# Copying and splitting a pair's first keys before, not after, the turning of its centroid products

## The chip, the cores and the metric

One NeuronCore of one Trainium2 chip runs the whole program. The metric is the device time of one execution in microseconds; the time of the kernel before is the median of three runs.

## The reference

A clustered attention, two batches of eight heads, 768 tokens and 64 features a head, is followed by two feed-forward networks. A query sees only the keys that fall to the same of 16 centroids.

```python
q_assign = argmax((q / |q|) @ (c / |c|).T)          # c: 16 centroids of the head
k_assign = argmax((k / |k|) @ (c / |c|).T)
mask = q_assign[:, :, :, None] == k_assign[:, :, None, :]
scores = where(mask, q @ k.T / sqrt(64), -1e9)
attn = softmax(scores) @ v
x = attn with the heads side by side                # 1536 x 512
h = relu(x @ w_in) ** 2 @ w_out                     # 512 -> 2048 -> 512
h = gelu_like(h @ w2_in) @ w2_out                   # 512 -> 2048 -> 512
```

All is float32. The kernel keeps that accuracy by splitting a factor into a high half in the fast format fp32r and a low half, the remainder.

## The kernel before

The heads are worked in eight pairs (pair 0 to pair 7), each pair two heads of the same batch. A pair has 12 steps of 128 query rows, six for each head, and the two heads alternate. One step multiplies a query tile with all 768 keys (`scores`, lines 620 and 623: the high halves against each other first, then the low halves together with 16 mask rows), takes the negative of the row maximum on VectorE (`peak`, line 629), the exponentials on ScalarE (`exponents`, line 637), turns them on TensorE (`turn`, line 645), copies them out of PSUM (`keep`, line 653, on ScalarE or VectorE) and multiplies them with the values (`values`, line 663). The scores have two PSUM buffers: a score needs the exponentials of the score two before it to be done. Most other products share a ring of four PSUM buffers.

While the steps of one pair run, the next pair is prepared (`prep`, from line 439). Its raw keys and queries come by DMA. Then:

- `square` (line 474, GpSimd) squares them, `aff` (lines 481 and 484, TensorE) multiplies with the centroids and sums the squares, `aff_out` (line 490, ScalarE) copies that out of PSUM.
- `back` (line 498, TensorE) transposes these centroid products, `back_out` (line 508, ScalarE) copies the transposes out.
- `root` (line 512, GpSimd) takes the square root of the norms, `inv_norm` (lines 518 and 519, VectorE) adds 1e-6 and inverts, `scale` (line 531, GpSimd) applies it, `most` (line 539, VectorE) takes the maximum over the centroids; `less`, `first`, `least`, `one_hot` (lines 542 to 557) make the assignment, `mask` (line 564) turns it, and DMAs lay it under the queries and keys.
- `k_high(j)` for head j of the pair (line 448, ScalarE) copies the keys into the high half and sends a copy of that by DMA to the other 64 partitions (line 449, SyncE's queue). `k_low(j)` (line 453, GpSimd) subtracts it from the raw keys. `q_high` (lines 458 and 459) and `q_low` (line 463) do the same for the queries. The buffers hold four heads, so the even head of pair p writes where the even head of pair p - 2 was read, by `scores`, to the end of that pair.

Beside this, the attention's results leave: `inverse`, `turn_sums` (lines 673 to 677, VectorE) and `send` (line 682, GpSimd, four small copies) bring the inverse row sums into a row, DMAs of lines 683 and 689 spread them, `whole` (line 722) applies them, `whole_high` and `whole_low` (lines 730 and 734) split the result, and `t_sum_first` (line 741, mostly GpSimd) adds results for the first network. From step 70 on, the networks' weights are decoded too (from line 266). Behind the attention the networks run on TensorE (lines 835, 912, 921 and 1024).

No scheduler decides the order. Each piece of work is put into a list with a number, its moment, by `at`, and the list is sorted; every engine then works its own share of it in that order, and waits where an operand isn't there yet:

```python
start = NQ * p                      # NQ = 12, one unit is one score
at(start + key, f, x)               # key from PAIR, for pairs 3 to 7
begin = ORIGIN + 2 * k              # scores 2k and 2k + 1; ORIGIN = -1.0
GROUP = dict(scores=(0.0, 0.3), peak=(0.5, 0.7), exp=(0.85, 1.5), turn=(2.64, 2.85, 3.06), ...)
for _, _, f in sorted(events, key=lambda e: e[:2]):
```

So the numbers of `PAIR` are moments of a pair's preparation, counted from the start of its own scores. Pair 2 takes `PAIR` too, with some moments of its own (`THIRD`: its `back` is at -15.1 and its `back_out` at -14.75 and -14.7). Pairs 0 and 1 have tables of their own.

Of the kernel before, what the change touches and what calls it, by code (L numbers as in the profile page):

```python
# [32 lines left out]
PAIR = dict(  # L33
    load_q=-20.601, load_k=-20.501, load_v=-5.2, square=(-16.9, -16.5),
    aff=(-15.15, -15.1), aff_out=(-14.95, -14.8), back=(-13.15, -13.1), back_out=(-12.95, -12.8),
    k_high=(-13.4, -6.9), k_low=(-12.95, -6.3), q_high=(-12.6, -10.7), q_low=(-12.2, -8.9),
    root=-12.7, inv_norm=-9.95, scale=-9.9, most=-8.98, less=-8.95, first=-6.98,
    least=-6.95, one_hot=-6.0, mask=(-5.15, -5.1), mask_out=(-4.95, -4.8),
)
# [8 lines left out]
    q_low=(-49.9, -49.8), k_low=(-47.95, -49.7),  # L48
# [8 lines left out]
    q_high=(-11.3, -6.18), q_low=(-10.1, -6.1), k_high=(-5.45, -4.75), k_low=(-5.4, -4.7),  # L57
# [1159 lines left out]
```

## Time and profile before

| | |
|---|---|
| median of three runs | 757.31 us (757.30 to 757.36) |
| the profiled execution | 757.72 us |
| its span, first to last instruction | 755.9 us |
| TensorE busy | 741.3 us, 98% of the span |
| VectorE busy | 530.5 us, 70% |
| ScalarE busy | 454.8 us, 60% |
| GpSimd busy | 173.0 us, 23% |
| granted TensorE clock | 1.00 |

Pair 2 is prepared from about 35 to 58 us of the span, pair 5 from about 124 to 147, pair 7 from about 183 to 210; the attention's steps end near 247 us. In the rows below PE is TensorE, PEld its weight load, DVE VectorE, ACT ScalarE and POOL GpSimd; "arena" is the SBUF area that holds nearly all tiles, and L518 is line 518. The spans of POOL are rough; starts are firmer than ends.

### The profile page before, as it was taken

To read this page: it belongs to the slowest core of one execution; us is meant where nothing else is said; L and a number is where in the kernel's file an instruction comes from. 1 tells how busy PE (TensorE), PEld (TensorE's weight loads), DVE (VectorE), ACT (ScalarE), POOL (GpSimd) and SP (SyncE) were. 2 spreads that over 40 slices of the span, in tenths; PEclk is the share of its full clock that TensorE was granted. 3 is DMA by queue.
4 is the path that set the end of the run, shared out by engine and by line. 5 is a ranking of instruction groups with operands and counts; after the bars stand their busy time and mean duration, and the time that the engine had idled before them with its cause. 6 is when DMAs were issued, how large, how long until landed. Compare 5 with 4: busy or idle time off the path is not lost.

```text
span 755.9 us, 10860 instructions
## 1 busy us (share of the span) xinstructions
PE 741.3 (98%) x3965; PEld 603.5 (80%) x3965; DVE 530.5 (70%) x954; ACT 454.8 (60%) x784; POOL 173.0 (23%) x186
## 2 busy tenths in 40 slices
PE   9899999999999999999999999999999999999998
PEld 6676676676666799999988888888888888888886
DVE  6877877977897667775787769754777677776321
ACT  7877768776777478776844435554656564443321
POOL 4765766785749130000000000000000000000000
PEclk9999999999999999999999999999999999999999
DMA  6143332333321121200232320100212212230301
GB/s 190 47 122 75 97 103 61 87 87 94 108 54 61 69 105 62 108 26 31 83 111 86 109 85 21 36 29 28 84 57 83 84 56 95 101 112 28 112 1 56
DMA packets 19481, 57.53 MB, mean 76 GB/s; under 512 B 3146, under 2 KB 5156, under 8 KB 18404
## 3 DMA queue, kind: packets, MB, share of 16 engines
q1 hardware_dynamic: 19140, 56.19, 23.5%
q8 instruction: 31, 0.51, 0.3%
q10 hardware_dynamic: 288, 0.66, 0.2%
q14 instruction: 22, 0.18, 0.1%
HBM read 45.97 MB, written 3.19 MB: 65 GB/s over the span
## 4 chain that ended last, share of the span: by engine, by line
PE 83%; DVE 7%; ACT 4%; POOL 3%; issue 1%; DVEq 0%; POOLq 0%; ACTq 0%
PE bank L1024 35%; PE row L835 13%; PE bank L912 10%; PE bank L921 6%; PE ps_v L663 5%; PE ps_p L645 5%; DVE arena L629 3%; PE ps_s L620 3%; ACT arena L637 3%; PE ps_s L623 2%; PE ps_aff L481 1%; DVE arena L518 1%; PE ps_h L835 1%; PE warm L397 1%; POOL arena L296 1%
## 5 line engine op out<-in xcount | busy, mean ns | idle before, releaser
L1024 PE MATMUL bank<-arena 128*128 128x512 f32 x1152 | 261.5, 389 | 0.0
L1024 PEld LDWEIGHTS bank<-arena 128*128 128x128 f32 x1152 | 216.1, 188 | 45.0 <-DVE arena L1011 0.2
L637 ACT ACTIVATE arena<-ps_s,arena 128x768 f32<-128x768 f32 x96 | 87.1, 907 | 46.0 <-DVE arena L629 45.9
L629 DVE TENSOR_SCALAR_CACHE_REDUCE arena<-ps_s 128x768 bf16<-128x768 f32 x96 | 91.7, 955 | 32.5 <-ACT arena L490 13.1
L1007 ACT CAST arena<-arena 128x512 fp32r<-128x512 f32 x96 | 59.5, 620 | 85.6 <-PE bank L1024 85.2
L835 PE MATMUL row<-arena 128*128 128x384 f32 x630 | 109.7, 334 | 0.4 <-ACT arena L853 0.4
L835 PEld LDWEIGHTS row<-arena 128*128 128x128 f32 x630 | 109.2, 188 | 0.7 <-ACT arena L853 0.7
L1011 DVE TENSOR_TENSOR arena<-arena,arena 128x512 fp32r<-128x512 f32 x96 | 66.1, 689 | 60.1 <-ACT arena L1007 59.9
L912 PE MATMUL bank<-arena 128*128 128x512 f32 x336 | 80.9, 389 | 0.0
L912 PEld LDWEIGHTS bank<-arena 128*128 128x128 f32 x336 | 63.1, 188 | 13.1
L663 PE MATMUL ps_v<-arena 128*64 128x384 f32 x384 | 72.3, 498 | 0.0
L645 PE MATMUL ps_p<-arena 128*128 128x128 f32 x576 | 70.8, 272 | 0.0
L244 ACT CAST arena<-arena 128x512 fp32r<-128x512 f32 x48 | 29.8, 620 | 64.6 <-DVE arena L240 64.5
L645 PEld LDWEIGHTS ps_p<-arena 128*128 128x128 f32 x576 | 65.8, 141 | 2.2 <-issue 0.6
L620 PE MATMUL ps_s<-arena 128*128 128x384 f32 x192 | 55.1, 368 | 7.0 <-ACT arena L637 6.6
L620 PEld LDWEIGHTS ps_s<-arena 128*128 128x128 f32 x192 | 30.9, 188 | 31.2 <-ACT arena L637 17.3
L247 DVE TENSOR_TENSOR arena<-arena,arena 128x512 fp32r<-128x512 f32 x48 | 33.2, 692 | 24.1 <-ACT arena L244 23.3
L623 PE MATMUL ps_s<-arena 80*128 80x384 f32 x192 | 49.8, 340 | 0.1
L921 PE MATMUL bank<-arena 128*128 128x512 f32 x192 | 48.1, 389 | 0.0
L653 DVE COPY arena<-ps_p 128x512 f32<-128x512 f32 x72 | 47.0, 678 | 0.3 <-PE ps_p L645 0.2
L663 PEld LDWEIGHTS ps_v<-arena 128*64 128x64 f32 x384 | 23.4, 136 | 25.5 <-issue 25.4
L653 ACT COPY arena<-ps_p 128x512 f32<-128x512 f32 x72 | 41.9, 582 | 0.5 <-PE ps_p L645 0.5
(140 smaller groups left out, 939.4 us busy)
## 6 DMA issues: line engine op xcount, KB each, us to landing
arena<-in_w_dram SPq DMA_DIRECT2D x48, 512.0 KB, 3.3
arena<-in_w_dram SPq DMA_DIRECT2D x8, 1024.0 KB, 4.8
arena<-arena SPq DMA_DIRECT2D x32, 192.0 KB, 2.6
arena<-in_k_t_dram SPq DMA_DIRECT2D x8, 384.0 KB, 4.9
arena<-in_v_dram SPq DMA_DIRECT2D x8, 384.0 KB
arena<-sums_d SPq DMA_DIRECT2D x30, 96.0 KB, 2.8
out_dram<-arena SPq DMA_DIRECT2D x11, 256.0 KB, 2.1
arena<-in_q_t_dram SPq DMA_DIRECT2D x7, 384.0 KB, 3.5
```

Of the source, the lines that this page charges most:

```text
L620: nc.tensor.matmul(ps[:, n, :HALF], lhsT=x_s[i][:, t * P:(t + 1) * P], rhs=k1_s[i][:, n * HALF:(n + 1) * HALF], start=True, stop=False)
L623: nc.tensor.matmul(ps[:, n, :HALF], lhsT=q2_s[i][:, t * P:(t + 1) * P], rhs=k2_s[i][:, n * HALF:(n + 1) * HALF], start=False, stop=True)
L629: nc.vector.tensor_scalar(out=unused, in0=s_t[g][:, :, :HALF], scalar1=-scale, scalar2=None, op0=ALU.mult, op1=ALU.min, accum_out=m_t[g])
L637: nc.scalar.activation(out=p_t[g].rearrange("p (n f) -> p n f", n=2), in_=s_t.pop(g)[:, :, :HALF], func=AF.Exp, bias=m_t.pop(g), scale=sca ...
L645: nc.tensor.transpose(ps[:, x * P:(x + 1) * P], p_t[2 * k + j][:, t * P:(t + 1) * P], ident)
L653: (nc.scalar.copy if on_act else nc.vector.tensor_copy)(out=pt_t[n][:, 4 * b:4 * b + 4, i * P:(i + 1) * P], in_=tp_t.pop((k, b)).rearrange ...
L663: nc.tensor.matmul(pv_t[n][j * D:(j + 1) * D, :HALF], lhsT=raw[n // 2, "v"][:, j, t, :], rhs=pt_t[n, j][:, t, :], start=(t == 0), stop=(t ...
L835: nc.tensor.matmul(ps, lhsT=w[:, a, (off + x) * P:(off + x + 1) * P], rhs=FIRST_MOVING[moving, b][x][:, e, :], start=(n == 0 and name in ( ...
L912: nc.tensor.matmul(ps, lhsT=w[:, a, off + x * P:off + (x + 1) * P], rhs=MOVING[moving][x][:, b, :], start=(n == 0 and name in ("P1", "P2", ...
L921: nc.tensor.matmul(ps, lhsT=w[:, a, kk * P:(kk + 1) * P], rhs=THIRD_CHUNK[kk][:, b, :], start=(n == 0), stop=(n == 11), skip_group_check=True)
L1011: nc.vector.tensor_tensor(out=t[:, 1, :], in0=g_t[m][:, c, :], in1=t[:, 0, :].bitcast(F32), op=ALU.subtract)
L1024: nc.tensor.matmul(ps, lhsT=lhsT, rhs=rhs, start=(m == 0 and e == 0), stop=(m == MF - 1 and e == 2))
```

## The change

Two numbers of `PAIR` change, each the moment of the pair's first head (j = 0):

```diff
 PAIR = dict(
-    k_high=(-13.4, -6.9), k_low=(-12.95, -6.3), q_high=(-12.6, -10.7), q_low=(-12.2, -8.9),
+    k_high=(-14.7, -6.9), k_low=(-14.6, -6.3), q_high=(-12.6, -10.7), q_low=(-12.2, -8.9),
```

`back` stands at -13.15 and -13.1, `back_out` at -12.95 and -12.8, `root` at -12.7. The queues of TensorE, VectorE and SyncE stay as they were. On ScalarE and GpSimd the rows of lines 448 and 453 move in pairs 2 to 7.

ScalarE, a preparation as in pairs 3 to 7, before (L490 `aff_out`, L637 exponentials, L653 `keep`, L448 `k_high`, L508 `back_out`, L458 `q_high`):

```order
L490 COPY arena_59<-ps_aff 128x384 x2
L637 ACTIVATE arena_59<-ps_s,arena_59 128x768
L653 COPY arena_59<-ps_p 128x4x128
L637 ACTIVATE arena_59<-ps_s,arena_59 128x768
L448 CAST arena_58<-arena_59 64x768
L653 COPY arena_59<-ps_p 128x4x128
L508 COPY arena_59<-ps_back 128x3x98 x2
L458 CAST arena_58<-arena_59 64x768
```

and now:

```order
L490 COPY arena_59<-ps_aff 128x384 x2
L448 CAST arena_58<-arena_59 64x768
L637 ACTIVATE arena_59<-ps_s,arena_59 128x768
L653 COPY arena_59<-ps_p 128x4x128
L637 ACTIVATE arena_59<-ps_s,arena_59 128x768
L653 COPY arena_59<-ps_p 128x4x128
L508 COPY arena_59<-ps_back 128x3x98 x2
L458 CAST arena_58<-arena_59 64x768
```

The cast of the keys now stands ahead of two exponentials and a copy that it stood behind. In pair 2 it stands between the two copies of line 508.

GpSimd at the same place of pair 5, before (L474 `square`, L734 `whole_low`, L741 `t_sum_first`, L682 `send`, L453 `k_low`, L512 `root`, L463 `q_low`, L531 `scale`):

```order
L474 TENSOR_TENSOR arena_59<-arena_59 128x768 x2
L734 TENSOR_TENSOR arena_58<-arena_59,arena_58 128x384
L741 TENSOR_TENSOR arena_59<-arena_59 128x384 x3
L682 COPY arena_59<-arena_59 6x32 x4
L453 TENSOR_TENSOR arena_58<-arena_59,arena_58 64x768
L512 TENSOR_TENSOR arena_59<-arena_59 128x24
L463 TENSOR_TENSOR arena_58<-arena_59,arena_58 64x768
L531 TENSOR_TENSOR arena_59<-arena_59 128x384
```

and now:

```order
L474 TENSOR_TENSOR arena_59<-arena_59 128x768 x2
L734 TENSOR_TENSOR arena_58<-arena_59,arena_58 128x384
L741 TENSOR_TENSOR arena_59<-arena_59 128x384 x3
L453 TENSOR_TENSOR arena_58<-arena_59,arena_58 64x768
L682 COPY arena_59<-arena_59 6x32 x4
L512 TENSOR_TENSOR arena_59<-arena_59 128x24
L463 TENSOR_TENSOR arena_58<-arena_59,arena_58 64x768
L531 TENSOR_TENSOR arena_59<-arena_59 128x384
```

The subtraction of line 453 went ahead of the four small copies of line 682, and the root follows these directly.

## Rows read from the trace of the kernel before

**Rows 1.** The page, part 1: busy us, share of the span, instructions of TensorE.

```profile
PE 741.3 (98%) x3965; PEld 603.5 (80%) x3965; DVE 530.5 (70%) x954; ACT 454.8 (60%) x784; POOL 173.0 (23%) x186
```

**Rows 2.** Waits of TensorE: waiter, releaser, us in total, times, longest.

```profile
PE ps_s L620 <- ACT arena L637: 6.6, 16, 0.9
```

**Rows 3.** Timeline of TensorE, pair 5: start, length, instruction, [idle before, releaser].

```profile
137.43 1.51 PE L663 MATMUL ps_v<-arena 128*64 128x384 f32 x8
138.87 0.61 PE L620 MATMUL ps_s<-arena 128*128 128x384 f32 x2
...
139.67 0.52 PE L620 MATMUL ps_s<-arena 128*128 128x384 f32 x2
...
141.78 1.51 PE L663 MATMUL ps_v<-arena 128*64 128x384 f32 x8
143.69 0.62 PE L620 MATMUL ps_s<-arena 128*128 128x384 f32 x2 [0.40 <-ACT arena L637]
...
145.06 0.62 PE L620 MATMUL ps_s<-arena 128*128 128x384 f32 x2 [0.41 <-ACT arena L637]
```

**Rows 4.** Chain of waits that ended last, same step: start, us, what.

```profile
138.05 1.73 DVE arena L518
...
142.65 0.99 ACT arena L637 x2
```

**Rows 5.** Timeline of GpSimd and VectorE, pair 5, ahead of that step.

```profile
130.56 0.96 POOL L682 COPY arena<-arena 6x32 f32<-6x32 f32 x4 [2.85 <-ACT arena L448]
131.61 1.82 POOL L453 TENSOR_TENSOR arena<-arena,arena 64x768 fp32r<-64x768 f32 x1
133.39 4.16 POOL L512 TENSOR_TENSOR arena<-arena 128x24 f32<-128x24 f32 x1
137.49 0.55 DVE L734 TENSOR_TENSOR arena<-arena,arena 128x384 fp32r<-128x384 f32 x1
137.63 2.10 POOL L463 TENSOR_TENSOR arena<-arena,arena 64x768 fp32r<-64x768 f32 x1
137.96 1.81 DVE L518 TENSOR_SCALAR arena<-arena 128x24 f32<-128x24 f32 x1
```

**Rows 6.** Timeline of ScalarE and TensorE, pair 5, around the cast's two places.

```profile
124.89 1.05 ACT L490 COPY arena<-ps_aff 128x384 f32<-128x384 f32 x2 [0.65 <-PE ps_aff L484]
125.32 0.62 PE L620 MATMUL ps_s<-arena 128*128 128x384 f32 x2
...
127.46 0.90 ACT L637 ACTIVATE arena<-ps_s,arena 128x768 f32<-128x768 f32 x1 [1.53 <-DVE arena L629]
...
129.71 0.82 ACT L448 CAST arena<-arena 64x768 fp32r<-64x768 f32 x1
...
130.91 0.70 ACT L508 COPY arena<-ps_back 128x294 f32<-128x294 f32 x2
```

**Rows 7.** Timeline: VectorE beside a long GpSimd operation, pairs 1 and 5.

```profile
28.30 1.81 POOL L463 TENSOR_TENSOR arena<-arena,arena 64x768 fp32r<-64x768 f32 x1 [0.86 <-ACT arena L458]
29.56 0.96 DVE L546 SCALAR_TENSOR_TENSOR arena<-arena 128x384 f32<-128x384 f32 x1
...
132.25 0.96 DVE L629 TENSOR_SCALAR_CACHE_REDUCE arena<-ps_s 128x768 bf16<-128x768 f32 x1
```

**Rows 8.** Timeline of GpSimd, VectorE and TensorE, pair 2.

```profile
45.09 4.17 POOL L512 TENSOR_TENSOR arena<-arena 128x24 f32<-128x24 f32 x1
...
48.71 0.55 DVE L734 TENSOR_TENSOR arena<-arena,arena 128x384 fp32r<-128x384 f32 x1
49.29 0.18 DVE L518 TENSOR_SCALAR arena<-arena 128x24 f32<-128x24 f32 x1
...
54.68 0.62 PE L620 MATMUL ps_s<-arena 128*128 128x384 f32 x2 [0.17 <-ACT arena L637]
```

**Rows 9.** Timeline of TensorE, pair 7.

```profile
204.95 0.61 PE L620 MATMUL ps_s<-arena 128*128 128x384 f32 x2 [0.95 <-ACT arena L637]
...
209.60 0.37 PE L564 MATMUL ps_oh<-arena 128*64 128x128 f32 x3 [0.63 <-DVE arena L653]
```

## The prediction

> **What bounds the kernel now.** I read the page first: TensorE is busy 741.3 of 755.9 us [rows 1], so a change elsewhere pays only where TensorE waits. The wait view says where that is [rows 2]: 6.6 us before scores (line 620), in 16 pieces, for the exponential (line 637) that still holds the PSUM buffer. TensorE's timeline of one pair shows the pattern [rows 3]. Without a wait the scores start 1.44 us after the start of the value products (137.43 to 138.87), and the second scores 0.80 us after the first (138.87 to 139.67). One step later these distances are 1.91 (141.78 to 143.69) and 1.37 (143.69 to 145.06). So pair 5 loses 0.47 + 0.57, about 1.05 us, in one step. Pairs 3, 4 and 6 have the same two waits of 0.40 to 0.41 us at their own times; pair 2 has a smaller first and pair 7 a larger second one [rows 8, 9].
>
> The chain of waits through that step says what is late [rows 4]: VectorE's tensor_scalar of line 518 (`inv_norm`) takes 1.73 us on the chain, then come its reciprocal, GpSimd's scaling (line 531), VectorE's maximum, the peak of the scores and, at 142.65, the exponential that TensorE waits for. Line 518 works on 24 numbers a partition. The timeline of GpSimd and VectorE [rows 5] says why it is slow: `q_low` (line 463) runs from 137.63 to 139.73, and line 518, due at 137.96, ends just behind it, at 139.77. `q_low` runs that late because the root before it (line 512, 4.16 us) started at 133.39, behind `k_low` (line 453). `k_low` waited its turn behind the copies of line 682 and took GpSimd from 131.61 to 133.39: 1.78 us, counted from start to start.
>
> **The change, part by part.** It adds and removes no work. In pairs 2 to 7 `k_high(0)` (0.82 us on ScalarE), the transfer that it issues and `k_low(0)` go ahead of the centroid transposes.
>
> ScalarE, new place. `k_high` stands behind the copies of line 490 and ahead of an exponential that ScalarE sits idle for: in pair 5 from 125.94 to 127.46 [rows 6]. In the built order it waits for the line 620 products of the last score that reads its buffer, and these start at 125.32 and take 0.62 us, so it can run from about 126.05 to 126.9. The exponential, which waits for VectorE until 127.46, is not touched: cost 0, with 0.55 us to spare. If that cover were gone, the exponential would start late; TensorE comes back to its buffer a step later, 4.35 us (137.43 to 141.78) after 125.32, at 129.67 at the earliest, and takes up a buffer 1.04 us after an exponential starts (142.65 to 143.69), here at 128.50. With the second exponential 1.37 behind, as the two waits of [rows 3] are apart, it would be 129.87 against 129.67 + 0.80 = 130.47. So TensorE would feel only what is beyond a further 0.6 us. In pair 2 the cast stands between the two copies of line 508; the second goes some 0.8 us later, which the root does not feel, since it follows line 682 there too.
>
> ScalarE, old place. 0.82 us at 129.71 falls away, and the copies of line 508, which release the root, end up to 0.8 us before 131.61. Worth nothing by itself.
>
> GpSimd, new place. In pair 5 GpSimd falls idle at 127.71, 2.85 us before line 682 starts at 130.56 on VectorE's transpose [rows 5]. `k_low` takes its 1.82 us there, to about 129.6: cost 0, with 0.96 us to spare. Pairs 3, 4 and 7 have more room: one operation of line 741 stands ahead and not three. Beside the old `k_low` VectorE's peak took its usual 0.96 us [rows 7], and beside the new one it does the same kind of work, so I charge nothing.
>
> SyncE. The transfer of line 449 keeps its place in the queue and is ready some 3.6 us sooner; what is queued behind it can only start sooner. Cost 0.
>
> GpSimd, old place: this carries the gain. Behind line 682 the root now follows at once, near 131.61 and not 133.39: 1.78 us earlier. It hands on 4.24 us after its start (133.39 to 137.63), so `q_low` runs from 135.85 to 137.67. VectorE comes to line 734 at 137.49, in the last 0.18 us of `q_low`. Such an operation is held by a running `q_low`: line 546 took 0.96 us beside one [rows 7], where line 734, which also has two inputs of that size, takes 0.55. So lines 734 and 518 start 0.18 late; line 518 then finds GpSimd idle and takes the 0.18 us that it took in pair 2, where it came first [rows 8]. Sooner by 1.81 - 0.18 - 0.18 = 1.45 us: line 531, the maximum, the peak and the exponential.
>
> What is late next. The first exponential at 141.20 lets TensorE go at 142.24, but that is busy with value products until 143.22 (141.78 + 1.44): the first wait is gone with 0.98 us to spare. The second scores could start at 145.06 - 1.45 = 143.61, and TensorE comes to them at 143.22 + 0.80 = 144.02: gone, with 0.41 to spare. So the whole 1.05 us comes back, and the rest of the shift turns into idle time of ScalarE.
>
> The Trainium skill (SBUF — State Buffer, Who interferes with whom) says that a VectorE operation with two SBUF inputs, or a tensor_scalar in a two-port mode, is blocked for the whole of a GpSimd operation that reads SBUF and began first. The trace agrees for `q_low`, but not for the root: line 734 of pair 2 took its 0.55 us at 48.71 with line 512 under way until 49.26 [rows 8]. By the rule the shift is the 1.45 us above; if the root's row were the general case, it would be 1.63, and with pairs 2 and 7 the sum below would be 6.6 us and not 6.25.
>
> Sum. Pairs 3 to 6: 4 x 1.05 = 4.2. Pair 2: its first wait of 0.17 costs 0.24 (0.07 more, as in pair 5), the second 0.57 as elsewhere. There `q_low` would now run from 47.55 (45.09 - 1.78 + 4.24) to 49.37 and hold line 734, due at 48.71, for 0.66 us, so less of the shift is left; between 0 and 0.81, I take 0.6, nearer the upper end since the shift of 1.78 outweighs the 0.66. Pair 7: its second wait of 0.95 costs 1.11 (0.16 more, as in pair 5), and later TensorE waits 0.63 on VectorE's queue [rows 9]; that queue goes early by the shift, so I take 1.45 (bounds 0.47, the first wait alone, and 2.2, all three). Together 6.25 us. Behind the attention TensorE's products set the pace, and all that feeds them stands in its queue behind the same scores, so the shift should reach the end. The profiled execution took 757.72 us (span 755.9), 0.41 above the median of 757.31: 757.72 - 6.25 = 751.47, as a median 751.06, rounded to 751.1.
>
> **The rivals.** (a) Only the first waits go. Something takes the 0.41 us of spare. The place for it: `k_low` ends later than computed, still runs when VectorE comes to the next small tensor_scalar (line 673, ahead of the transpose that line 682 waits for) and holds it as `q_low` holds line 518 [rows 5]; then line 682 and the root go late as well. At the worst the second waits (0.57 x 4, and 0.6 in all in pairs 2 and 7) come back: 6.25 - 2.9 = 3.4, or 754.0. For it: the spare is less than a third of the shift. Against it: what I shift are the same instructions at the same distances.
>
> (b) Nothing is gained, because the root's start is set by something else near 133.4, or line 518 meets another GpSimd operation: 757.3. Against it: line 682 (130.56 + 0.96) and line 508 (130.91 + 0.70) are both done by 131.61, and in the built order nothing else stands ahead of the root.
>
> (c) Slower: `k_high` is not free at 126.05. If it were released as late as it stood before, at 129.71 (by a transfer that still uses its buffer, say), ScalarE would stand in front of the exponential until 130.53, TensorE would get the buffer at 131.57 and not 129.67, and the second wait would add 0.57: up to 2.5 us in each of six pairs, 15 us, 772. It decides from a release near 127.2 on. Against it: the keys were loaded long before, and the score that it waits for is the one whose exponential comes next.
>
> (d) More comes back: pair 7 loses all three waits and pair 2 both, 4.2 + 0.81 + 2.2 = 7.2, or 750.1.
>
> **How the numbers follow.** The forecast of 751.1, with its own range of 750.3 to 752.2, has 0.72; (a) 0.12; (d) and a little beyond it 0.03; (b) 0.08; (c) 0.05. The range runs from (d) to (a), 750.0 to 754.0, with some 0.85 in it. A measurement of this kernel can tell about 0.2%, 1.5 us, from no change. Faster: 0.72 + 0.12 + 0.03 = 0.87; within 0.2%: 0.08; slower: 0.05.
>
> **What would show it.** In the changed profile: `k_high(0)` in ScalarE's gap, and the exponential behind it as soon after its peak as before; `k_low` done before line 682; the root right behind line 682; line 518 at about 0.18 us in pairs 3 to 7; no wait of line 620 for line 637 in pairs 3 to 6. Wrong would be: a root that starts no earlier, line 518 still at 1.8 us, an exponential pushed behind `k_high`, or an attention shorter by 6 us that the products behind it give back.

## The result and the profile after

The changed kernel takes 750.28 us (median of five runs, 750.11 to 750.53), the kernel before 757.33 (757.30 to 757.66): a ratio of 0.9906, 95% interval 0.9892 to 0.9921, 7.05 us less. Predicted were 751.1 and a range of 750.0 to 754.0. The profiled execution took 750.53 us, with a span of 748.7 and a granted clock of 0.999.

The page, part 1 of after, answers to [rows 1], and the waits of TensorE to [rows 2]:

```profile
PE 738.9 (99%) x3965; PEld 603.4 (81%) x3965; DVE 523.0 (70%) x954; ACT 455.9 (61%) x784; POOL 171.3 (23%) x186
```

```profile
PE ps_s L620 <- ACT arena L637: 1.4, 4, 0.4
PE ps_oh L564 <- DVE arena L653: 0.6, 1, 0.6
```

The 6.6 us in 16 pieces have become 1.4 us in 4. Three of the four lie in the preparation of pair 1, at 24.13, 27.54 and 31.21, the last (0.17 us) at 216.94; the change touches neither place. The second row is the wait of the mask transposes in pair 7, which [rows 9] also show.

VectorE is 7.5 us less busy with the same instructions. Line 518 is where that went (five executions, one in each of pairs 3 to 7, are 1.64 us shorter; 0.48 us come in again at line 734 of pair 2). Its own view (least, median and longest of 8, in ns):

```profile
L518 DVE TENSOR_SCALAR arena<-arena x8: 166/171/179, 9.7 to 191.4; 128x24 f32<-128x24 f32 x8
```

Before, most of them took 1.81 us, as in [rows 5]. The timeline of pair 5 shows each link of the chain. By then all stands 3.37 us earlier than before (the scores at 125.32 in [rows 6] start at 121.95), so 3.37 is added to compare. ScalarE, answering to [rows 6]:

```profile
121.52 1.04 ACT L490 COPY arena<-ps_aff 128x384 f32<-128x384 f32 x2 [0.87 <-PE ps_aff L484]
122.60 0.84 ACT L448 CAST arena<-arena 64x768 fp32r<-64x768 f32 x1
124.10 0.90 ACT L637 ACTIVATE arena<-ps_s,arena 128x768 f32<-128x768 f32 x1 [0.66 <-DVE arena L629]
```

The cast sits in the idle time, and ScalarE still waits 0.66 us for VectorE behind it. GpSimd and VectorE, answering to [rows 5]:

```profile
124.08 1.81 POOL L453 TENSOR_TENSOR arena<-arena,arena 64x768 fp32r<-64x768 f32 x1
...
126.49 0.17 DVE L673 TENSOR_SCALAR arena<-arena 128x6 f32<-128x6 f32 x1 [0.76 <-ACT arena L637]
...
127.20 0.93 POOL L682 COPY arena<-arena 6x32 f32<-6x32 f32 x4 [1.30 <-DVE arena L677]
128.21 4.16 POOL L512 TENSOR_TENSOR arena<-arena 128x24 f32<-128x24 f32 x1
132.45 1.81 POOL L463 TENSOR_TENSOR arena<-arena,arena 64x768 fp32r<-64x768 f32 x1
134.13 0.55 DVE L734 TENSOR_TENSOR arena<-arena,arena 128x384 fp32r<-128x384 f32 x1
134.60 0.17 DVE L518 TENSOR_SCALAR arena<-arena 128x24 f32<-128x24 f32 x1
135.25 0.84 POOL L531 TENSOR_TENSOR arena<-arena 128x384 f32<-128x384 f32 x1 [0.99 <-DVE arena L519]
```

`k_low` ends at 125.89, 0.60 us before VectorE comes to line 673. Line 682 stands where it stood (127.20 + 3.37 = 130.57 for 130.56), the root follows it, `q_low` is over when line 518 comes, and line 518 takes 0.17 us.

TensorE in the same step, answering to [rows 3]:

```profile
138.42 1.51 PE L663 MATMUL ps_v<-arena 128*64 128x384 f32 x8
139.86 0.61 PE L620 MATMUL ps_s<-arena 128*128 128x384 f32 x2
...
140.66 0.52 PE L620 MATMUL ps_s<-arena 128*128 128x384 f32 x2
```

The distances are 1.44 and 0.80 us, those of a step without a wait.

Where the 7 us come from is read by setting the start times of all 96 score groups (line 620) of the two traces side by side:

| place | start of the first scores | start of the second scores | up to the next scores | together |
|---|---|---|---|---|
| pair 2 | 0.24 | 0.57 | 0.11 | 0.92 |
| each of pairs 3 to 6 | 0.47 to 0.48 | 0.57 | 0.22 to 0.23 | 1.27 to 1.28 |
| pair 7 | 0.47 | 1.12 | | 1.59 |

That is 7.6 us in all. The traced run of after began its attention 0.2 us late, which another run of the same kernel (the last experiment) did not; steps of 0.06 us and less elsewhere make that good. At the last scores TensorE is 7.62 us ahead (242.40 to 234.78), and it is 7.65 ahead when the last output's transfer is issued (752.14 to 744.49); nothing is given back in the networks. The span keeps only 7.2 us of it, since it ends 4.23 us after that issue and 3.80 after it before. Each trace of this case shows one of these two tails: 3.80 or 3.81 in four of them, one of which has the early places (the cast twice), and 4.23 or 4.24 in the other eight, one of which has no gain (only the cast ahead). So the tail does not follow the change.

### The profile page after: what moved, and what is told of

Read it like the earlier page. It is cut to its first block, busy times and chain, and to the rows that moved or that the text cites. A ratio compares the mean times of both kernels' runs of the same rounds, so it can differ in the third digit from the quotient of the medians.

```text
span 748.7 us, 10861 instructions
## 1 busy us (share of the span) xinstructions
PE 738.9 (99%) x3965; PEld 603.4 (81%) x3965; DVE 523.0 (70%) x954; ACT 455.9 (61%) x784; POOL 171.3 (23%) x186
## 4 chain that ended last, share of the span: by engine, by line
PE 92%; DVE 3%; ACT 3%; POOL 1%; issue 1%; DVEq 0%; POOLq 0%; ACTq 0%
PE bank L1024 35%; PE row L835 13%; PE bank L912 10%; PE ps_v L663 8%; PE ps_p L645 7%; PE bank L921 6%; PE ps_s L620 4%; PE ps_s L623 4%; DVE arena L629 1%; PE ps_aff L481 1%; ACT arena L637 1%; PE ps_h L835 1%; PE warm L397 1%; POOL arena L296 1%; DVE arena L653 1%
## 5 line engine op out<-in xcount | busy, mean ns | idle before, releaser
L637 ACT ACTIVATE arena<-ps_s,arena 128x768 f32<-128x768 f32 x96 | 87.1, 907 | 36.1 <-DVE arena L629 35.9
L912 PEld LDWEIGHTS bank<-arena 128*128 128x128 f32 x336 | 63.1, 188 | 13.1
L653 DVE COPY arena<-ps_p 128x512 f32<-128x512 f32 x72 | 47.0, 678 | 0.3 <-PE ps_p L645 0.2
L653 ACT COPY arena<-ps_p 128x512 f32<-128x512 f32 x72 | 41.9, 582 | 0.5 <-PE ps_p L645 0.5
```

Of the source, the lines that this page charges most:

```text
L637: nc.scalar.activation(out=p_t[g].rearrange("p (n f) -> p n f", n=2), in_=s_t.pop(g)[:, :, :HALF], func=AF.Exp, bias=m_t.pop(g), scale=sca ...
L653: (nc.scalar.copy if on_act else nc.vector.tensor_copy)(out=pt_t[n][:, 4 * b:4 * b + 4, i * P:(i + 1) * P], in_=tp_t.pop((k, b)).rearrange ...
L912: nc.tensor.matmul(ps, lhsT=w[:, a, off + x * P:off + (x + 1) * P], rhs=MOVING[moving][x][:, b, :], start=(n == 0 and name in ("P1", "P2", ...
```

## The experiments

Edits are given against the changed kernel. My theory: in pairs 3 to 7 the whole gain comes from line 518 no longer running beside `q_low` (pair 2, where line 518 was fast before, is taken up in the next section). Rivals: relief of ScalarE at the cast's old place; an earlier root as such; and, for the places used, that one of them has no cover.

**Only the cast goes ahead; `k_low` stays at its old moment.**

```diff
-    k_high=(-14.7, -6.9), k_low=(-14.6, -6.3),
+    k_high=(-14.7, -6.9), k_low=(-12.95, -6.3),
```

> Only `k_high(0)` moves; `k_low(0)` stays between line 682 and the root. Theory (the gain is GpSimd's 1.78 us ahead of the root): no gain, 757.3 within 0.7; line 453 starts behind line 682 as before, line 518 takes 1.8 us in pairs 3 to 7 and TensorE's waits of 0.4 us stay. Rival (the 0.82 us that leave ScalarE's busy place, with line 508 sooner, are a good part of it): 2 us or more faster, 755 or less.

Measured: 758.1 us beside 757.56 for the kernel before, ratio 1.0007 (0.9998 to 1.0016). TensorE's waits and line 518 are as before:

```profile
PE ps_s L620 <- ACT arena L637: 6.5, 16, 1.0
```

```profile
L518 DVE TENSOR_SCALAR arena<-arena x8: 178/1808/1812, 9.4 to 196.9; 128x24 f32<-128x24 f32 x8
```

The relief of ScalarE is worth nothing.

**The root early, but `q_low` still on line 518:** `k_low` between the root and `q_low`.

```diff
-    k_low=(-14.6, -6.3),
+    k_low=(-12.4, -6.3),
```

> `k_high(0)` as in the change, `k_low(0)` between the root and `q_low(0)`. The root starts 1.78 us earlier, as in the change, but `q_low` stands where it stood before, on line 518. Narrow theory (the meeting costs): no gain, line 518 at 1.8 us, 757.3 within 0.7. Rival (the earlier root is the gain): as the change, 750.3.

Measured: 758.5, ratio 1.0014 (1.0004 to 1.0023). GpSimd and VectorE in pair 5:

```profile
131.86 4.16 POOL L512 TENSOR_TENSOR arena<-arena 128x24 f32<-128x24 f32 x1
135.99 1.81 POOL L453 TENSOR_TENSOR arena<-arena,arena 64x768 fp32r<-64x768 f32 x1
137.87 2.14 POOL L463 TENSOR_TENSOR arena<-arena,arena 64x768 fp32r<-64x768 f32 x1
...
138.25 1.80 DVE L518 TENSOR_SCALAR arena<-arena 128x24 f32<-128x24 f32 x1
```

The root follows line 682 as in the change, and nothing is gained. An earlier root as such is out. Pair 2 confirms it from the other side: there line 518 took 0.18 us before [rows 8] and now meets `q_low`, takes 1.81 us at 49.28, and the scores behind it come 0.62 us late, a good part of what this run is over the kernel before.

**The root late, but `q_low` off line 518:** the kernel before, with only `q_low` moved behind the scaling.

```diff
-    k_high=(-14.7, -6.9), k_low=(-14.6, -6.3), q_low=(-12.2, -8.9),
+    k_high=(-13.4, -6.9), k_low=(-12.95, -6.3), q_low=(-9.85, -8.9),
```

> The order before, with one move: `q_low(0)` goes behind the scaling of line 531. Root and `k_low(0)` start as late as before (root near 4.2 us before line 734's turn). Theory in its narrow form (not the root's start but the meeting of `q_low` with line 518 is what costs): line 518 at 0.18 us, as fast as the second experiment, 752.3 to 754.3. Rival (the root is late and has to start earlier): no gain, 757.3.

Measured: 756.09, ratio 0.9983 (0.9973 to 0.9992). TensorE's waits, and VectorE and GpSimd in pair 5:

```profile
PE ps_oh L564 <- DVE arena L557: 2.8, 6, 1.8
PE ps_oh L564 <- DVE arena L653: 1.6, 6, 0.8
PE ps_s L620 <- ACT arena L637: 1.4, 4, 0.4
```

```profile
136.07 0.17 DVE L518 TENSOR_SCALAR arena<-arena 128x24 f32<-128x24 f32 x1
...
140.47 1.83 POOL L463 TENSOR_TENSOR arena<-arena,arena 64x768 fp32r<-64x768 f32 x1
141.24 1.48 DVE L546 SCALAR_TENSOR_TENSOR arena<-arena 128x384 f32<-128x384 f32 x1
```

With the root as late as ever, line 518 is at 0.17 and the score waits of pairs 2 to 7 are gone: meeting `q_low` is what cost. But the second head's `q_low` is now pushed onto line 546 (1.48 us for 0.55), and the mask transposes wait for lines 557 and 653 instead. So the size was missed (752.3 to 754.3 were expected): against the change each of pairs 2 to 6 loses 0.57 us at the mask, and pair 7 loses 3.3, which the next run explains.

**`k_low` behind the scaling,** `q_low` left alone.

```diff
-    k_high=(-14.7, -6.9), k_low=(-14.6, -6.3),
+    k_high=(-13.4, -6.9), k_low=(-9.85, -6.3),
```

> `k_high` as before; `k_low(0)` goes the other way, behind the scaling of line 531. The root follows line 682 as in the change. Theory: line 518 at 0.18 us and both first waits gone, but GpSimd does 1.82 us more before line 542, so `q_low(1)` runs when VectorE comes to line 546 and holds it about 0.9 us, and the wait ahead of the mask's transposes stays or grows: 3 to 5 us faster, 752.3 to 754.3. Rival (the early place in GpSimd's idle time, or the early transfer, is what pays): 757.

Measured: 756.28, ratio 0.9982 (0.9973 to 0.9992). Line 518 at 0.17 and no score wait left in pairs 2 to 7, as expected, but the size was missed: each of pairs 3 to 6 loses 0.50 us of it again at the mask, pair 2 0.71 and pair 7 3.5. In pair 5 GpSimd's two halves follow one another up to line 546, which takes 1.24 us at 141.54. In pair 7 they meet steps of the weight decoder on VectorE (lines 273 and 276), and more follows. The last row is a stretch of 3 us, with the busy times of TensorE, its weight loads, VectorE, ScalarE and GpSimd, then the granted clock, the DMA share and GB/s:

```profile
201.41 1.77 DVE L276 TENSOR_SCALAR arena<-arena 128x512 int32<-128x512 int32 x1
...
205.77 0.35 PE L564 MATMUL ps_oh<-arena 128*64 128x128 f32 x3 [1.82 <-DVE arena L557]
```

```profile
208.00:211.00 3.00, 3.00 (x15) 2.90 (x14) 2.87 (x7) 1.66 (x4) 1.61 (x5) 0.50 0.28 54
```

Line 276 takes 0.42 us alone and 1.77 here, beside line 453 (201.09 to 202.90). TensorE waits 1.82 and 0.77 us for the mask and is busy for 0.47 of the 3 us from 204 to 207. From 208 to 211 its granted clock is 0.50, the level of 1.2 GHz, and 1.00 before and behind. Counted by the score starts, 2.1 us go at the mask and 1.6 us in the stretch at half clock. The run with `q_low` behind the scaling shows the same stretch and the same 1.6 us; in all other traces the clock is 1.00 from the first scores to the last product.

The slot that the change uses, ahead of line 682, is the one of the four tried that pushes no long GpSimd operation onto a short VectorE one in pairs 3 to 7; in pair 2 it costs 0.48 us at line 734.

**The cast twice** in its new place (the second writes the same again):

```diff
-                    nc.scalar.copy(out=t[o:o + D], in_=raw[p, "k"][o:o + D])
+                    for _ in range(2 if p > 1 and j == 0 else 1):
+                        nc.scalar.copy(out=t[o:o + D], in_=raw[p, "k"][o:o + D])
```

> The change, with `k_high(0)` done twice in its new place in pairs 2 to 7. Theory: ScalarE is idle 0.66 us behind the cast in pair 5; the second cast of 0.83 us makes the exponential 0.2 us late, within the 0.6 us that TensorE doesn't feel: 750.3 within 0.7. Rival (the place ahead of the exponential has no cover): 0.8 us in each of six pairs, 755.

Measured: 750.8, ratio 0.9909 (0.9895 to 0.9922), no difference from the change that is clear of the noise. In pairs 3 to 7 ScalarE's place has room for 0.84 us more. In pair 2, where the cast stands between the two copies of line 508, it has not: the second copy comes later, the twelve turns behind (line 646 in this kernel) take 1.83 us for 1.48, and the next scores are 0.36 us late.

```profile
38.33 1.83 PE L646 MATMUL ps_p<-arena 128*128 128x128 f32 x12
```

**`k_low` twice** in its new place:

```diff
-                    (nc.vector if start_up else nc.gpsimd).tensor_tensor(
-                        out=k2_s[i][:D], in0=raw[p, "k"][o:o + D], in1=..., op=ALU.subtract)
+                    for _ in range(2 if p > 1 and j == 0 else 1):
+                        (nc.vector if start_up else nc.gpsimd).tensor_tensor(
+                            out=k2_s[i][:D], in0=raw[p, "k"][o:o + D], in1=..., op=ALU.subtract)
```

> The change, with `k_low(0)` done twice in its new place in pairs 2 to 7 (the second writes the same values). It tests rival (a). Theory: in pairs 5 and 6, where three operations of line 741 stand ahead, the second one ends about 0.5 us after line 682's turn and holds the small tensor_scalar of line 673 about 1.2 us; line 682 and the root go 1.2 us late, which is more than the spare of the second wait (139.00 + 1.05 against 140.66: 0.6 us). Pairs 3, 4 and 7 begin 1 us earlier and lose nearly nothing. Together 1.5 to 2.5 us slower than the change: 751.8 to 752.8. Rival (GpSimd's idle time and the spare cover it all): 750.3. If VectorE's queue is hit in all six pairs: 754 or more.

Measured: 754.21, ratio 0.9954 (0.9941 to 0.9968): 3.9 us of the gain lost. That is the third case named: VectorE's queue is hit in all six pairs (line 673 held for 0.60 to 1.38 us), where the theory had put it in two. GpSimd and VectorE in pair 5 (the lines of this kernel stand one higher: 674 is `inverse`, 735 `whole_low`, 464 `q_low`):

```profile
125.35 3.72 POOL L454 TENSOR_TENSOR arena<-arena,arena 64x768 fp32r<-64x768 f32 x2
...
127.57 1.54 DVE L674 TENSOR_SCALAR arena<-arena 128x6 f32<-128x6 f32 x1 [0.76 <-ACT arena L638]
...
130.65 4.16 POOL L513 TENSOR_TENSOR arena<-arena 128x24 f32<-128x24 f32 x1
134.89 1.81 POOL L464 TENSOR_TENSOR arena<-arena,arena 64x768 fp32r<-64x768 f32 x1
135.21 1.91 DVE L735 TENSOR_TENSOR arena<-arena,arena 128x384 fp32r<-128x384 f32 x1
```

One hold begets the next. `k_low` holds the six numbers of `inverse` for 1.37 us (1.54 for 0.17), the transpose, line 682 and the root go late by as much, and `q_low` then holds `whole_low` for 1.36 us (1.91 for 0.55). In pairs 3 and 4 `k_low` had started earlier; the same rows of VectorE there:

```profile
70.28 0.82 DVE L674 TENSOR_SCALAR arena<-arena 128x6 f32<-128x6 f32 x1 [0.76 <-ACT arena L638]
77.92 1.20 DVE L735 TENSOR_TENSOR arena<-arena,arena 128x384 fp32r<-128x384 f32 x1
...
98.93 0.77 DVE L674 TENSOR_SCALAR arena<-arena 128x6 f32<-128x6 f32 x1 [0.76 <-ACT arena L638]
106.57 1.15 DVE L735 TENSOR_TENSOR arena<-arena,arena 128x384 fp32r<-128x384 f32 x1
```

So one run gives three sizes of the same delay, and the kernel before a fourth. Against the scores of the change:

| VectorE's chain late by | lost up to the second scores | from there to the next scores | together |
|---|---|---|---|
| 0.60 (pair 4) | 0.00 | 0.22 | 0.22 |
| 0.65 (pair 3) | 0.05 | 0.22 | 0.27 |
| 1.36 (pair 5) | 0.76 | 0.22 | 0.98 |
| 1.63 (before, pair 5) | 1.04 | 0.23 | 1.27 |

The last column is the first less 0.37, within 0.01. In these four cases TensorE loses what the chain is late, less about 0.37 us of spare.

**The wait that is left in pair 7.** VectorE's copy of line 653, which the mask transposes wait 0.61 us for, stands behind a step of the weight decoder (line 280). Three kernels try to take it away; the change is measured again with the last two:

```diff
-PAIR_0 = dict(..., steps=(76.3, 77.0, 77.3, 78.0, 78.6, ...), rest=(82.2, 82.6, 83.3, 85.0, 85.4))
+PAIR_0 = dict(..., steps=(76.3, 77.0, 77.3, 78.7, 79.1, ...), rest=(82.2, 83.05, 83.3, 85.0, 85.4))
```

Both edits:

> The change, with two more moves at the end of the attention. In pair 7 the weight decoding of line 280 goes behind the copy of line 653 that TensorE's mask transposes wait for (0.61 us there), and GpSimd's line 291 goes behind line 682, since it held line 673 for 1.0 us. Theory: the wait of 0.61 goes and so does one of 0.17: 0.6 to 0.9 us faster than the change, 749.4 to 749.7. Rival: GpSimd's chain of weights and splits, 2 us later, becomes late for the first network's products: 750.3 or more.

Measured: 751.46, ratio 0.9922 (0.9908 to 0.9936), 1.2 us over the change's 750.28: the wait is gone, and 1.7 us are lost between 202 and 222 us. Only the `steps`:

> The change with VectorE's two pieces of the next weights' generator (lines 280 and 284, planned at 78.0 and 78.6) planned at 78.7 and 79.1, so that in pair 7 the mask copy of line 653 goes ahead of line 280. Nothing else moves. In the run that moved these two together with the raw low half, the 0.61 us wait of the mask transposes at 202 us was gone and 1.7 us were lost later, between 208 and 222 us. Theory A, the late loss belongs to the raw low half alone: the 0.6 us stay, 0.6 us less than the change in the same call, about 749.7 where the change has 750.3, and no wait of the score products between 210 and 225 us. Theory B, the later steps delay the generator's chain and with it the widening in pair 7: the late waits are there too and the time is 1 us over the change, about 751.4.

Measured: 750.42, ratio 0.9906 (0.9890 to 0.9923). Only the `rest`:

> The change with only the raw low half of pair 7's preparation (GpSimd line 291) moved behind the four small copies of line 682. In the change line 673 of VectorE takes 1.01 us at 212.10 beside line 291, where it takes 0.17 alone. Theory A: line 673 back at 0.17, but lines 291 and 296 end 0.9 us later, ScalarE's line 299 waits for 296 with the exponentials of line 637 behind it, and the score products wait for these: 1.7 us slower than the change, about 752.0, with the mask wait of 0.61 still at 202 us. Theory B, the loss came from the generator's steps: no late waits, equal to the change or up to 0.8 us faster (750.3 to 749.5).

Measured: 751.37, ratio 0.9919 (0.9904 to 0.9934). And the change itself:

> The changed kernel itself, as the measure for the two others of this call. 750.3 us, 7 us less than before.

Measured: 750.12, ratio 0.9902 (0.9887 to 0.9916).

Of the 1.7 us, 1.1 belong to the `rest` edit: alone it costs that much of TensorE's time, 1.25 in the medians. The other 0.6 are what the `steps` edit wins at the mask and loses again. ScalarE and TensorE with the `rest` edit:

```profile
218.53 1.04 ACT L299 CAST arena<-arena 128x1024 fp32r<-128x1024 f32 x1 [1.84 <-POOL arena L296]
...
219.89 0.89 ACT L637 ACTIVATE arena<-ps_s,arena 128x768 f32<-128x768 f32 x1
...
220.93 0.62 PE L620 MATMUL ps_s<-arena 128*128 128x384 f32 x2 [1.10 <-ACT arena L637]
```

GpSimd's sums (line 296) end later, ScalarE waits 1.84 us for them with an exponential queued behind, and the scores wait for that. The hold that the edit removes (line 673 takes 1.0 us beside line 291 in the change, 0.17 here) had cost less.

Of the `steps` edit neither theory held: no late wait came, and the 0.6 us did not stay. ScalarE and TensorE with it, and TensorE in the change measured beside it:

```profile
209.85 0.84 ACT L288 CAST arena<-arena 128x768 fp32r<-128x768 f32 x1
210.58 0.91 ACT L637 ACTIVATE arena<-ps_s,arena 128x768 f32<-128x768 f32 x1
...
211.69 0.59 PE L620 MATMUL ps_s<-arena 128*128 128x384 f32 x2 [0.58 <-issue]
```

```profile
201.55 0.37 PE L564 MATMUL ps_oh<-arena 128*64 128x128 f32 x3 [0.59 <-DVE arena L653]
...
211.69 0.59 PE L620 MATMUL ps_s<-arena 128*128 128x384 f32 x2 [0.30 <-issue]
```

Both reach the same moment. TensorE is 0.64 us ahead from the mask on, and has lost all of it by these scores. They start 1.11 us after an exponential that starts at 210.58 (210.59 in the change). Its own maximum was there at 209.87 (209.88); what it stands behind is ScalarE's queue, which has no pause from 208.49 on: the exponential before, a copy of line 653 and the cast of line 288. The exponential at 208.49 (208.50) had waited 2.08 us for VectorE's maximum, which starts at 207.44 (207.45). So the moment is set by VectorE up to that maximum and by ScalarE behind it. The busy times with the edit (columns as above):

```profile
197.00:211.00 14.00, 13.93 (x91) 9.77 (x90) 13.16 (x29) 10.09 (x20) 4.57 (x7) 1.00 0.35 73
```

VectorE works from 197.74 to 210.48 with no pause over 0.13 us. Its queue in another order lets the mask go earlier, but the work up to that maximum is the same. Less work on VectorE ahead of it, or line 288 behind the exponential, might bring a part of the 0.6 us. Neither was tried, and no version beat the change.

## Why the prediction was right, and where its sizes were off

**The mechanism held at every step that it named.** In before's time, predicted and found in pair 5: cast free to run at 126.05, found 125.97; root near 131.61, found 131.58; `q_low` from 135.85, found 135.82; VectorE at line 734 at 137.49, found 137.50; line 518 at 0.18, found 0.17. The undoing runs show that each half of the reason is needed: `k_low` moved where `q_low` stays on line 518 gives nothing, `q_low` moved away from it takes the score waits away though the root is late.

**The shift was 1.63 us, not 1.45.** What was mis-sized is the 0.18 us for which I let `q_low` hold line 734: it was nothing. Line 734 started 0.13 us before `q_low`'s recorded end (132.45 + 1.81 = 134.26) and took its plain 0.55. Line 531 came at 135.25 + 3.37 = 138.62 where it came at 140.25. This alone changed no term, because the score waits of pairs 3 to 6 were gone with 1.45 too.

**A third loss of each pair was not seen.** "So the whole 1.05 us comes back" was too little by 0.22: between the second scores and the next ones as much was lost again. No row of the waits showed it, since it lay inside two groups. The second scores after the wait take 0.61 or 0.62 us where those of the change take 0.52, which is 0.09 at the next start. The other 0.13 are in the mask transposes. VectorE and TensorE in pair 4, before and after:

```profile
118.63 0.69 DVE L653 COPY arena<-ps_p 128x512 f32<-128x512 f32 x1
119.06 0.69 PE L564 MATMUL ps_oh<-arena 128*64 128x128 f32 x6
119.59 0.56 PE L620 MATMUL ps_s<-arena 128*128 128x384 f32 x2
```

```profile
115.05 0.68 DVE L653 COPY arena<-ps_p 128x512 f32<-128x512 f32 x1
115.83 0.55 PE L564 MATMUL ps_oh<-arena 128*64 128x128 f32 x6
116.23 0.56 PE L620 MATMUL ps_s<-arena 128*128 128x384 f32 x2
```

The copy that frees a buffer of the ring ended 0.26 us after the six transposes began, and now ends 0.10 before; the next scores follow 0.40 us behind the first transpose and not 0.53. The two runs with late halves show this place as an open wait of 0.17 us for line 653, cut into two groups of three. Four pairs of 0.22 and the 0.11 of pair 2 are 1.0 us of the 1.3 by which the sum (6.25 for 7.6) fell short; this term of the sum was the one most in error. The table of the doubled `k_low` shows that this loss answers to the same delay: with a chain late by 0.6 us it is nearly the only one. That the total is off by 0.8 us only (751.1 for 750.28) is in part luck: 0.4 us of TensorE's lead went into the longer tail of that execution. The result lies just below the forecast's own range (750.3 to 752.2) and inside the full one (750.0 to 754.0).

**Pair 2: 0.92 for 0.6.** Both its waits went (0.80), though `q_low` did hold line 734 there, as I had worked out:

```profile
47.68 1.81 POOL L463 TENSOR_TENSOR arena<-arena,arena 64x768 fp32r<-64x768 f32 x1
48.88 1.03 DVE L734 TENSOR_TENSOR arena<-arena,arena 128x384 fp32r<-128x384 f32 x1
```

The hold is 0.48 us (1.03 for 0.55), not 0.66. What I had taken from the shift was too much, and line 518 is not the reason here, since it took 0.18 us before: the scaling waits at 50.48 for VectorE, at 51.24 before for GpSimd, and stands 0.93 us sooner once the 0.17 us that after runs late there is taken off.

**Pair 7: 1.59 for 1.45.** The two score waits of [rows 9] went whole; the mask's wait stayed (0.61 for 0.63). I had let a part of it go, since "that queue goes early by the shift". VectorE is full there, and TensorE came to the mask sooner by as much as the copy. The two score waits alone were 0.47 + 1.11 = 1.58 in my own numbers, so 1.45 undercut them although a part of the mask's wait was meant to go as well. It was a value chosen between bounds; that it came within 0.14 us is luck.

**The rivals.** (a) did not come about, but its mechanism is real. With `k_low` doubled, the hold on line 673 delays line 682 and the root, as it was described, and takes back 3.9 us of about 7. It was nearer than the 0.96 us of room that I named: what counts is the 0.60 us from `k_low`'s end to line 673, not the time to line 682. (b) is excluded by the trace. (c) likewise: the cast ran at once, and in pairs 3 to 7 a second one beside it costs nothing. (d) came nearest in time, 750.1, but by another way: not by pair 7's third wait, but by the third waits of the others.

The Trainium skill (SBUF — State Buffer, Who interferes with whom) says that VectorE's two-input operations and two-port tensor_scalars stand blocked while an earlier GpSimd operation reads SBUF. The runs agree for lines 453 and 463 in each meeting shown above, with lines 518, 546, 673 and 734. For the root (line 512) there is only the meeting of [rows 8], which disagrees. Two runs repeat it in the same place, and line 734 takes 0.55 us again (at 48.37 with only the cast moved, at 48.58 with only `q_low` moved); why the root differs is not shown.

## What to carry to other kernels

Look for a VectorE operation on a few numbers that takes as long as a GpSimd operation beside it, and move the GpSimd one to a slot in which VectorE does no such work; then ask which short VectorE operation it meets in the new slot, since the other three of the four slots tried here put a long operation onto a short one, and even the fourth does in pair 2. When a chain comes earlier, follow it to all who use it, and compare distances between start times with those of a step without waits: a wait inside a group of instructions has no row of its own. A wait that vanishes by reordering a queue that is full to the next join is paid again there.

## What the runs showed of the hardware that I had not expected

The hold ends ahead of the GpSimd operation's recorded end, by the same amount in every such meeting of the twelve traces. A held line 734 ended 0.41 to 0.42 us after the recorded end of `q_low` where it takes 0.55 when free: at 137.12 for 136.70 in pair 5 with `k_low` doubled, at 49.91 for 49.49 in pair 2 of the change, at 79.12 for 78.70 in pair 3 with `k_low` doubled. So it is let go some 0.13 us before that end, and an overlap of 0.13 or less in the records, as in pair 5 of the change, costs nothing. The held tensor_scalars agree: line 674 ended at 129.11, 0.04 us after the 129.07 of `k_low`, and takes 0.17 alone.
